# Linear attention followed by an MLP mixer on one core: the first channel product of 8 of 9 chunks in Strassen's form, smaller attention rings, new order lists

## The chip, the core and the metric

The kernel runs on one core of a Trainium2 chip. The core has five engines that take instructions from queues of their own, each queue in order: TensorE (PE, with its weight loads shown as PEld), VectorE (DVE), ScalarE (ACT), GpSimd (POOL) and SyncE (SP, here for issuing DMAs alone). Matrix products land in PSUM, of which there are eight banks of 128 partitions by 512 float32; DVE and ACT read PSUM, POOL is given SBUF operands only in this kernel. The metric is the device time in microseconds of one execution.

## What is computed

```python
def phi(x):                                   # x is q or k, scaled by D**-0.25
    h = einsum('bhsd,md->bhsm', x, omega) - sum(x*x, -1, keepdims=True)/2
    return exp(h - max(h, -1, keepdims=True)) / sqrt(m)
q_p, k_p = phi(q_s), phi(k_s)
kv, z = einsum('bhsm,bhsd->bhmd', k_p, v), sum(k_p, axis=2)
attn = einsum('bhsm,bhmd->bhsd', q_p, kv) / (einsum('bhsm,bhm->bhs', q_p, z)[..., None] + 1e-6)
x = attn.transpose(0, 2, 1, 3).reshape(B, S, H*D)          # 8 x 576 x 512
h = maximum(x^T @ w_tok1, 0) @ w_tok2                      # token mix, 576 -> 256 -> 576
u = x + h^T
out = u + maximum(u @ w_ch1, 0) @ w_ch2                    # channel mix, 512 -> 1536 -> 512
```

There are 8 batches, 8 heads, 576 rows, a head size of 64 and 128 features.

## The kernel before

**Tiling.** A batch has 576 rows: 512 main rows and a tail of 64. The channel mix works on nine chunks of 512 rows: chunks 0 to 7 are the main rows of the batches, chunk 8 (`c == B`) is the eight tails together. All matrix operands are float16, sums are float32 in PSUM.

**Attention** (`attention`, by head pairs `hp`). `kp` (L657) and `qp` (L669) make the projections into two banks each; ACT takes the exponential into `kp`, `qp` (L515). DVE takes the row maximum of the k features (`km`, L681) and its reciprocal (L683), POOL scales v by it (`vs`, L295), PE forms kv (L702 and, for the tails, L709 or L711), which is copied to `kvsb` (L286). `num` (L735, L737) is the product with q; DVE divides (L744, L745) and writes `x`. Batches 0 and 1 get q and k by PE transposes of rows loaded as they are; the others go through a DRAM scratch (POOL's DMA queue) and come back by transposing DMAs on SP's queue into the rings `qT` and `kT`.

**Token mix** (`token_mix`; `token_mix_first` for batch 0). Two products (L778, L791) with a ReLU between; DVE adds x into `u` (L794), and one transposing DMA on SP's queue (L799) makes `uT`, the moving operand of the channel mix.

**Channel mix** (`channel_mix`). The first product runs over 12 blocks of 128 columns of `w_ch1`: each block is four matmuls of 128x512 into one bank (L967) and one ReLU from PSUM into `r3`, on ACT (L290) or DVE (L292). The second product of chunks 1 to 8 is in Strassen's form already (`channel_out_fast`, seven products of half size, L917): DVE forms eight sums of `r3` a chunk (L295, 768 columns each), PE runs 84 matmuls of 128x256 a chunk, and DVE reads the banks X, Y, Z seven times into the float32 `o` (L906). Four combinations `T1..T4` of blocks of `w_ch2` are made once by DVE (L448). Chunk 0 is plain (L1001).

**Order and places.** Each piece of work is a job: an engine, a cost, a function, what it depends on and which ring places it takes and gives back. The list `ORDER` was written out beforehand: `Planner.run` calls the jobs in that order, so it fixes the order on every engine's queue. `SLOT` gives the place in a ring that each job takes (the eight PSUM banks are one such ring), `MOVED` says which jobs run on another engine than their usual one, and a negative number in `ORDER` is a matmul on zeros into a bank (L1039), done in the first microseconds only.

Of the kernel before, what the change touches and what calls it, by code (L numbers as in the profile page):

```python
# [9 lines left out]
FP32 = mybir.dt.float32  # L10
# [110 lines left out]
class Planner:  # L121
# [41 lines left out]
    def engine(self, usual):  # L163

        return MOVED.get(len(self.jobs), usual)
# [3 lines left out]
def kernel(  # L169
# [51 lines left out]
    NH = NCB // 2  # L221
    DH = DM // 2
    t_S = sb([P, 3, NH, 2 * P], FP16, "S")
    t_T = sb([P, 4, NH, DH], FP16, "T")
    early = t_S.rearrange("p a b c -> p (a b c)")
    zeros = early[:, 0:SM]
    ident32 = early[:, SM : SM + 2 * P].bitcast(FP32)
# [844 lines left out]
```

## Time and profile before

The time is 283.71 us, the median of three runs (283.15 to 284.58). One execution was profiled; its page gives a span of 281.1 us from the first to the last instruction. The page says nothing of that execution's time outside the span.

| | before |
|---|---|
| time, median of 3 runs | 283.71 us |
| span of the profiled execution | 281.1 us |
| instructions | 6278 |
| PE busy | 270.3 us, 96% |
| DVE busy | 222.4 us, 79% |
| ACT busy | 138.6 us, 49% |
| POOL busy | 92.0 us, 33% |
| DMA moved | 39.66 MB |

How to read it: busy time is the time in which at least one instruction of an engine was in work. A group of instructions is named by line, engine, operation, the tiles written and read, and shape; behind the count stand the busy time and the mean length of one in ns, then the idle time just ahead of them and who ended it. PE's matmuls are pipelined: the length of one is longer than the pace of many, so their pace is taken from a run of them in the chain of waits, which follows the work back from the last instruction.

### The profile page before, as it was taken

The page shows a single profiled execution, that of the slowest core. Times are in us where ns is not written, and L with a number is a line of the kernel's source. Part 1 is how long each engine was busy: PE and PEld are TensorE (multiplying, and loading weights), DVE is VectorE, ACT ScalarE, POOL GpSimd, SP SyncE. Part 2 cuts the span into 40 slices and gives each one's busy share as a digit, 9 for nine tenths or more (in the row PEclk, how much of TensorE's full clock was granted, in tenths as well). Part 3 has the DMA queues.
Part 4 walks back from the last instruction along what each step waited for, and adds up shares of the span by engine and source line. Part 5 has one row for each costly group of instructions (what it writes and reads, how often), then busy time and mean ns, then how long its engine had stood idle before and what let it go on. Part 6 is the DMA issues. An engine that isn't in the chain of part 4 may idle for free.

```text
span 281.1 us, 6278 instructions
## 1 busy us (share of the span) xinstructions
PE 270.3 (96%) x2526; PEld 167.6 (60%) x2526; DVE 222.4 (79%) x462; ACT 138.6 (49%) x288; POOL 92.0 (33%) x116
## 2 busy tenths in 40 slices
PE   6899999999999999999999999999999999999993
PEld 2547546443657755665667647755676467446782
DVE  2589828499999899996997999977995893565992
ACT  1498994049676418743758445734753510031200
POOL 8574994007510872048008710510033000000001
PEclk9999999999999999999999999999999999999999
DMA  6999999999998999997979993960151304030125
GB/s 161 194 189 161 157 169 213 178 191 202 179 218 184 148 172 186 181 198 104 212 178 185 241 135 101 161 156 2 76 97 59 111 0 96 0 149 2 75 90 135
DMA packets 80524, 39.66 MB, mean 141 GB/s; under 512 B 63984, under 2 KB 76016, under 8 KB 80304
## 3 DMA queue, kind: packets, MB, share of 16 engines
q0 software_dynamic: 31744, 17.74, 44.1%
q1 hardware_dynamic: 46832, 15.77, 29.1%
q10 hardware_dynamic: 1920, 5.77, 5.4%
q8 instruction: 19, 0.31, 0.4%
q14 instruction: 9, 0.07, 0.1%
HBM read 35.95 MB, written 16.52 MB: 187 GB/s over the span
## 4 chain that ended last, share of the span: by engine, by line
PE 89%; DVE 3%; DMA 2%; ACT 2%; issue 0%; SPq 0%; DVEq 0%
PE bank L967 32%; PE bank L917 26%; PE bank L791 5%; PE bank L778 5%; PE bank L1001 4%; PE bank L735 3%; PE bank L657 3%; PE bank L702 3%; DMA wc<-in_k_dram 2%; PE bank L669 2%; ACT kp L515 1%; PE bank L845 1%; PE bank L817 1%; PE bank L737 1%; PE bank L771 1%; DVE T L448 1%
## 5 line engine op out<-in xcount | busy, mean ns | idle before, releaser
L967 PE MATMUL bank<-uT,wc 128*128 128x512 f16 x376 | 89.6, 379 | 0.5 <-DVE r L292 0.4
L290 ACT ACTIVATE r<-bank 128x512 f16<-128x512 f32 (+1 forms) x86 | 47.7, 601 | 82.7 <-PE bank L967 61.5
L295 POOL TENSOR_TENSOR vs<-v,vs 128x512 f16<-128x512 f16 x32 | 34.2, 1072 | 94.4 <-DVE vs L683 51.3
L967 PEld LDWEIGHTS <-wc 128*128 128x128 f16 x424 | 38.8, 98 | 38.8 <-issue 1.6
L917 PEld LDWEIGHTS <-r 128*128 128x128 f16 x384 | 36.8, 98 | 8.2 <-issue 1.1
L515 ACT ACTIVATE kp<-bank 128x512 f16<-128x512 f32 x64 | 36.7, 618 | 8.9 <-PE bank L657 7.1
L515 ACT ACTIVATE qp<-bank 128x512 f16<-128x512 f32 x64 | 36.7, 614 | 8.8 <-PE bank L669 5.8
L681 DVE TENSOR_REDUCE km<-kp 128x8 f16<-128x1024 f16 x32 | 38.7, 1208 | 1.2 <-ACT kp L515 1.1
L292 DVE TENSOR_SCALAR r<-bank 128x512 f16<-128x512 f32 (+1 forms) x40 | 26.3, 670 | 15.7 <-PE bank L967 11.3
L745 DVE TENSOR_TENSOR x<-bank,rc 128x320 f16<-128x320 f32 x62 | 30.5, 492 | 2.1
L917 PEld LDWEIGHTS <-S 128*128 128x128 f16 x288 | 28.1, 98 | 5.8 <-issue 0.3
L906 DVE TENSOR_TENSOR o<-u,bank 128x512 f32<-128x512 f16 x28 | 19.0, 679 | 6.2 <-PE bank L917 5.8
L917 PE MATMUL bank<-T,r 128*128 128x256 f16 x192 | 23.8, 273 | 0.0
L917 PE MATMUL bank<-wc,r 128*128 128x256 f16 x192 | 23.6, 273 | 0.0
L917 PE MATMUL bank<-T,S 128*128 128x256 f16 x192 | 23.4, 273 | 0.0
L946 POOL DMA_DIRECT2D out_dram<-o x2 | 1.3, 645 | 61.2 <-issue 61.2
L906 DVE TENSOR_TENSOR o<-o,bank 128x512 f32<-128x512 f32 (+1 forms) x27 | 16.6, 617 | 2.5 <-PE bank L917 1.8
L735 PEld LDWEIGHTS <-qp 128*128 128x128 f16 x256 | 13.5, 98 | 8.1 <-DVE kvsb L286 0.7
L794 DVE TENSOR_TENSOR u<-x,bank 128x512 f16<-128x512 f16 x28 | 17.6, 680 | 0.0
L735 PE MATMUL bank<-kvsb,qp 128*128 128x65 f16 x256 | 15.0, 193 | 0.5 <-DVE kvsb L286 0.5
L791 PE MATMUL bank<-r,w 128*128 128x512 f16 x56 | 14.1, 381 | 0.0
L744 DVE RECIPROCAL rc<-bank 128x5 f32<-128x5 f32 x62 | 11.4, 184 | 2.9 <-PE bank L737 2.2
(119 smaller groups left out, 379.0 us busy)
## 6 DMA issues: line engine op xcount, KB each, us to landing
out_dram<-o ACTq DMA_DIRECT2D x9, 512.0 KB, 2.7
q<-in_q_dram POOLq DMA_DIRECT2D x6, 576.0 KB, 9.7
wc<-in_moe_w_ch_dram POOLq DMA_DIRECT2D x4, 768.0 KB, 9.0
k<-in_k_dram POOLq DMA_DIRECT2D x6, 512.0 KB, 7.8
v<-in_v_dram POOLq DMA_DIRECT2D x6, 512.0 KB, 9.9
out_dram<-o SPq DMA_DIRECT2D x5, 512.0 KB, 3.9
r<-in_q_dram POOLq DMA_DIRECT2D x4, 288.0 KB, 7.5
v<-in_v_dram POOLq DMA_DIRECT2D x4, 256.0 KB, 8.1
```

Of the source, the lines that this page charges most:

```text
L290: nc.scalar.activation(out=out, in_=in_, func=AF.Relu)
L292: nc.vector.tensor_relu(out=out, in_=in_)
L295: (nc.gpsimd if eng == "POOL" else nc.vector).tensor_tensor(**kw)
L515: nc.scalar.activation(out=out, in_=in_, func=AF.Exp, bias=0.0, scale=1.0)
L681: nc.vector.reduce_max(out=mx, in_=kpv, axis=AX.X)
L735: nc.tensor.matmul(ps[:, k, j * 65 : (j + 1) * 65], st, s[:, i, 0 : D + 1], start=True, stop=True)
L745: nc.vector.tensor_tensor(out=t_x[place("x", b)][:, :, (2 * hp + hs[0]) * D : (2 * hp + hs[0] + n) * D].rearrange("p j (i d) -> p i j d", ...
L791: nc.tensor.matmul(ps, w2_of(tb, j), r1[:, tb, :], start=(tb == 0), stop=(tb == NT - 1))
L794: nc.vector.tensor_tensor(out=t_u[place("u", b)][:, j, :], in0=t_x[place("x", b)][:, j, :], in1=bank(n), op=ALU.add)
L906: nc.vector.tensor_tensor(out=o, in0=a, in1=ps, op=ALU.add)
L917: nc.tensor.matmul(ps[:, j * DH : (j + 1) * DH], a[:, cb, j * P : (j + 1) * P], w[:, cb, :], start=(bank_of(b, j0) not in held and j == j0 ...
L967: nc.tensor.matmul(ps, wc1[:, db, cb * P : (cb + 1) * P], moving(db), start=(db == 0), stop=(db == ND - 1))
```

## The change

The first channel product of chunks 1 to 8 is put in Strassen's form as well (`channel_in_fast`). Rows and inner index are halved: `uT` gives four blocks, `w_ch1` gives four. Three sums of blocks of `uT` go to a new tile `V`, a fourth replaces a block of `uT`. For each of three groups `p` of two column blocks, seven products (28 matmuls of 128x256) go to three banks X, Y, Z. X is read three times on the way into float32 tiles `s` (ring of four), and three more instructions add `s` to a bank and write `r3`; the ReLU of these three quarters then runs in place on `r3`, the fourth quarter's reads the bank.

```diff
+def channel_in_fast(c, key, jt):
...
+    sums = {}
+    for n, what, op, after in (
+        (1, lambda: (v_of(0), u_of(0, 1), u_of(0, 0)), ALU.subtract, ()),
+        (2, lambda: (v_of(1), u_of(1, 1), v_of(0)), ALU.subtract, (1,)),
+        (4, lambda: (v_of(2), u_of(1, 0), v_of(1)), ALU.subtract, (2,)),
+        (3, lambda: (u_of(0, 1), u_of(1, 1), u_of(0, 1)), ALU.subtract, (1,)),
+    ):
...
+            o, a, b = what()
+            tt(e_sum, out=o, in0=a, in1=b, op=op)
+        sums[n] = add(e_sum, 1.0, key - 0.2, go_u, deps=[*jt, *[sums[x] for x in after]], take=[("V", c)], give=own)
+    ops = {
+        1: ("X", A11, lambda: u_of(0, 0), [], True), 2: ("Y", A12, lambda: u_of(1, 0), [], True),
+        6: ("X", S2, lambda: v_of(1), [sums[2], j_W[2]], False), 5: ("Z", S1, lambda: v_of(0), [sums[1], j_W[1]], True),
+        7: ("X", S3, lambda: u_of(0, 1), [sums[3], j_W[3]], False), 3: ("Z", S4, lambda: u_of(1, 1), [j_W[4]], False),
+        4: ("X", A22, lambda: v_of(2), [sums[4]], False),
+    }
+    for p in range(NH // 2):
...
+                ps, m = bank(bank_of(b)), moving()
+                for t in range(2):
+                    cb = 2 * p + t
+                    for k in range(2):
+                        nc.tensor.matmul(ps[:, 2 * P * t : 2 * P * t + 2 * P], a[:, k, cb * P : (cb + 1) * P], m[:, :, k, :],
+                                         start=(begin and t == 0 and k == 0), stop=False, skip_group_check=True)
...
+            def go_k():
+                copy(e_k, t_s[place("s", (c, p, x))].rearrange("p (t s) -> p t s", t=2), seen("X"))
...
+            def go_t():
+                nc.vector.tensor_tensor(out=rows(i, e), in0=t_s[place("s", (c, p, x))].rearrange("p (t s) -> p t s", t=2), in1=seen(b), op=ALU.add)
...
+        p1 = product(1, [])
+        ka = kept("a", [p1])
+        p2 = product(2, [])
+        p5 = product(5, [])
+        summed("a", "Y", 0, 0, [ka, p2], True)
+        p6 = product(6, [ka])
+        kb = kept("b", [p6])
+        p7 = product(7, [kb])
+        kc = kept("c", [p7])
+        t22 = summed("c", "Z", 1, 1, [kc, p5], False)
+        p3 = product(3, [t22])
+        summed("b", "Z", 1, 0, [kb, p3], True)
+        p4 = product(4, [kc])
...
+        def go_r(e_r=e_r, rows=rows, seen=seen):
+            relu_to(e_r, rows(0, 1), seen("X"))
...
+                x = t_r3[place("r3", c)][:, NH * e + part.start : NH * e + part.stop, 2 * P * i : 2 * P * i + 2 * P]
+                if e_p == "POOL":
+                    nc.gpsimd.tensor_scalar_max(out=x, in0=x, scalar1=0.0)
+                else:
+                    relu_to(e_p, x, x)
+    return ready
```

Weights: four combinations of `w_ch1` (`first_weights`: `S1`, `S2`, `S4` in a new tile `W`, `S3` over a block of `w_ch1`) and four of `w_ch2` (`second_weights`, `T3` now over a block of `w_ch2`), each one instruction of 1536 columns on DVE or POOL. Those that overwrite wait until chunk 0's plain products have read the block. `T1`, `T2` and `T4` lie where the masked v tails of batches 0 and 1 lay, and the sums for the second product lie where early constants lay; both now wait for those readers by dependencies of their own.

```diff
+def first_weights(plain):
+    for n, out_, a, b, op in ((1, S1, A21, A22, ALU.add), (2, S2, S1, A11, ALU.subtract), (4, S4, A12, S2, ALU.subtract), (3, S3, A11, A21, ALU.subtract)):
...
+            tt(e_w, out=o, in0=a, in1=b, op=op)
...
-        for g in range(2):
-            part = slice(g * NH // 2, (g + 1) * NH // 2)
+    PARTS = (slice(0, 4), slice(4, NH))
...
+        for g, part in enumerate(PARTS):
...
-                e_sum = engine("DVE")
+                e_sum = engine("DVE", "POOL")
```

The sums ahead of the second product are cut 1024 and 512 columns wide, not 768 and 768, may run on POOL, and each depends on the quarters of `r3` it reads, not on all. The rings of `qT`, `kT` and `v` go from three to two places, those of `qp` and `kp` from four to three; the load of `w_ch2` is written behind the first transposes of k, whose rows lie in its tile. `ORDER`, `SLOT` and `MOVED` are new throughout, so the DMAs on POOL's queue also stand in another order.

```diff
-    COUNT = {"qT": 3, "kT": 3, "v": 3, "vt": 2, "qp": 4, "kp": 4, "vs": 4, "qpt": 2, "kpt": 2, "vbd": 2,
-             "kvsb": 3, "ktt": 2, "x": 3, "r1": 3, "u": 3, "uT": 3, "r3": 2, "S": 1, "o": 2, "bank": 8}
+    COUNT = {"qT": 2, "kT": 2, "v": 2, "vt": 2, "qp": 3, "kp": 3, "vs": 4, "qpt": 2, "kpt": 2, "vbd": 2,
+             "kvsb": 3, "ktt": 2, "x": 3, "r1": 3, "u": 3, "uT": 3, "V": 1, "s": 4, "r3": 2, "S": 1, "o": 2, "bank": 8}
```

What the two programs hold, counted from their instructions:

| | before | after |
|---|---|---|
| matmuls, first channel product, chunks 1 to 8 | 384 of 128x512 | 672 of 128x256 |
| DVE: ReLU of 512 columns from PSUM (L292) | 38 | 11 |
| DVE: copies of a bank to `s`; `s` + bank to `r3` | 0; 0 | 12; 72 |
| DVE: sums for the second product | 64 of 768 | 7 of 1024, 14 of 512 |
| DVE: sums of blocks of `uT`; of weights (1536) | 0; 4 | 14; 4 |
| DVE: ReLU in place | 0 | 8 of 1024, 8 of 512 |
| ACT: ReLU of 512 from PSUM; copies to `s`; ReLU in place | 84; 0; 0 | 39; 60; 7 of 1024, 6 of 512 |
| POOL: sums for the second product | 0 | 25 of 1024, 18 of 512 |
| POOL: sums of blocks of `uT`; of weights (1536) | 0; 0 | 18; 4 |
| POOL: ReLU in place | 0 | 9 of 1024, 10 of 512 |
| POOL: v scaled (`vs`) | 32 | 31 (one on DVE) |

More of the change, by code (lines that the diff above doesn't have):

```diff
@@ L104 @@
+"ACT", 1432: "SP",
 }
@@ L490, in row_transposes @@
         for o in range(2):
-            eng = engine("ACT" if on_act else "DVE")
+            eng = engine(*("ACT", "DVE") if on_act else ("DVE", "ACT"))
             def rows_out(o=o, eng=eng):
@@ L543, in attention @@
         if b == 1:
-            e_ktt = engine("POOL")
+            e_ktt = engine("POOL", "DVE")
             def k_tails():
@@ L627, in attention @@
         if b == 0:
-            e_dup = engine("POOL")
+            e_dup = engine("POOL", "DVE")
             def qt_dup():
@@ L779, in token_mix @@
             j1 = add("PE", mm(4, 512), key + step * tb * 0.2, t1, deps=[jt, j_w1], take=[("r1", b)])
-            e_relu = engine("ACT" if tb == 0 or BY["re1"] == "A" else "DVE")
+            e_relu = engine("ACT", "DVE")
             def relu(tb=tb, n=n, e_relu=e_relu):
@@ L942, in channel_out_fast @@
                 for h in range(2):
[L943 removed]
+                    eng = engine(*("POOL", "ACT", "SP") if need == "22" else ("ACT", "SP") if h else ("SP", "ACT"))
                     def store(i=i, j0=js[0], js=slice(*js), cols=cols, h=h, eng=eng):
@@ L957, in moving @@
+    def channel_mix(c, key, jt):
+        if c == NPE - 1:
+            first_weights(j_plain["in"])
+            second_weights(j_plain["out"])
+        if c >= NPE - 1:
+            channel_out_fast(c, key, channel_in_fast(c, key, jt))
+            return
         def moving(db):
-            return (t_uT[place("uT", c)] if c < B else uTt)[:, :, db, :]
+            return t_uT[place("uT", c)][:, :, db, :]
         jr = [None] * NCB
-        fast = c >= NPE - 1
-        order = [x for i in range(NH) for x in (i, i + NH)] if fast else range(NCB)
@@ L962, in channel_mix @@
-        for pos, cb in enumerate(order):
+        j_plain.update({"in": [], "out": []})
+        for pos, cb in enumerate(range(NCB)):
             n = ("h3", c, cb)
@@ L980, in channel_mix @@
                 j1 = add("PE", mm(4, 512), key + 0.5 * pos / NCB, c1, deps=[*jt, j_wc1[cb // (NCB // 2)], *first], take=[("bank", n), ("r3", c)],
-                       give=[("uT", c)] if c < B else [])
+                       give=[("uT", c)])
             j1.heavy = True
-            e_relu = engine("ACT" if c >= NPE or BY[("r0", "r1")[c]][cb] == "A" else "DVE")
+            j_plain["in"].append(j1)
+            e_relu = engine("ACT", "DVE")
             def relu(cb=cb, n=n, e_relu=e_relu):
@@ L1003, in channel_mix @@
                            deps=[prev, *jr[4 * part : 4 * part + 4], *j_wc2], take=[("bank", n)], give=[("r3", c), ("uT", c)])
+                j_plain["out"].append(prev)
             k2 = key + 0.5 + 0.5 * (3 * j + 3) / 12
-            e_out = engine("DVE")
+            e_out = engine("DVE", "ACT")
             def out_copy(j=j, n=n, e_out=e_out):
```

176 lines of the change are left out of this document (117 added, 59 removed), and 110 rows, old and new, of the table ORDER.

## The prediction

> **What bounds the kernel now.** I read the page's busy times first, then the chain of waits, then busy times by stretch.
>
> ```profile
> PE 270.3 (96%) x2526; PEld 167.6 (60%) x2526; DVE 222.4 (79%) x462; ACT 138.6 (49%) x288; POOL 92.0 (33%) x116
> PEclk9999999999999999999999999999999999999999
> ...
> PE 89%; DVE 3%; DMA 2%; ACT 2%; issue 0%; SPq 0%; DVEq 0%
> PE bank L967 32%; PE bank L917 26%; PE bank L791 5%; PE bank L778 5%; PE bank L1001 4%; PE bank L735 3%; PE bank L657 3%; PE bank L702 3%; DMA wc<-in_k_dram 2%; PE bank L669 2%; ACT kp L515 1%; PE bank L845 1%; PE bank L817 1%; PE bank L737 1%; PE bank L771 1%; DVE T L448 1%
> ```
>
> TensorE is busy 96% of the span at the full granted clock and makes up 89% of the chain that ended last; a third of the chain is the line that the change rewrites, L967. VectorE is second, 79% in the mean. A mean hides stages, so I asked for stretches: the head, the middle up to the last batch's `u`, its fullest 30 us, the last stretch and the end.
>
> ```profile
> core 0: us, PE busy (x) PEld busy (x) DVE busy (x) ACT busy (x) POOL busy (x), PEclk, DMA share, GB/s
> 0.00:33.50 33.50, 28.23 (x398) 17.31 (x399) 22.68 (x57) 22.71 (x55) 23.91 (x37) 1.00 1.05 172
> 65.00:95.00 30.00, 29.59 (x286) 18.49 (x286) 28.33 (x53) 21.14 (x44) 11.45 (x14) 1.00 1.07 188
> 230.00:276.40 46.40, 46.23 (x330) 31.99 (x327) 31.24 (x59) 5.92 (x11) 1.28 (x2) 1.00 0.22 68
> 276.40:281.10 4.70, 0.00 (x0) 0.00 (x0) 0.29 (x1) 0.00 (x0) 0.00 (x0) 0.88 0.51 142
> 33.50:230.00 196.50, 195.79 (x1800) 118.30 (x1800) 168.22 (x348) 109.98 (x223) 66.79 (x78) 1.00 0.89 153
> ```
>
> In the middle PE never rests (195.79 of 196.5 us) and DVE has 168.22, or 86%; in the fullest 30 us DVE stands at 28.33, or 94%, with PE still at 99%. So PE sets the pace, and DVE has only 28 us to spare over the whole middle. That reserve decides this case.
>
> **What it takes from PE.** The pace of matmuls comes from long unbroken runs in the chain:
>
> ```profile
> 238.88 13.81 PE bank L967 x64
> ...
> 265.73 10.52 PE bank L917 x96
> ```
>
> ```profile
> L967 PE MATMUL bank<-uT,wc 128*128 128x512 f16 x376 | 89.6, 379 | 0.5 <-DVE r L292 0.4
> L917 PEld LDWEIGHTS <-r 128*128 128x128 f16 x384 | 36.8, 98 | 8.2 <-issue 1.1
> ```
>
> A 512-column matmul costs 13.81/64 = 0.2158 us, a 256-column one 10.52/96 = 0.1096 us. The change takes out 384 x 0.2158 = 82.9 us and puts in 672 x 0.1096 = 73.6 us: 9.2 us less on PE. There are 288 more weight loads, but one takes 98 ns, under the 109.6 ns of the matmul that hides it, and L917's run shows that pace with one load per matmul. If that cover were gone, each load would show in full (28 us), which L917 excludes. PE alone would give 281.1 - 9.2 = 271.9 us of span.
>
> **What it gives to DVE.** DVE instructions overlap at their ends, so I take their pace from the gaps between starts in a stretch without idle time:
>
> ```profile
> 225.93 0.56 DVE L295 TENSOR_TENSOR S<-r,S 128x768 f16<-128x768 f16 x1
> 226.40 0.55 DVE L295 TENSOR_TENSOR S<-S,r 128x768 f16<-128x768 f16 x1
> ...
> 226.93 0.69 DVE L906 TENSOR_TENSOR o<-u,bank 128x512 f32<-128x512 f16 x1
> 227.53 0.55 DVE L295 TENSOR_TENSOR S<-r,S 128x768 f16<-128x768 f16 x1
> 228.00 1.87 DVE L794 TENSOR_TENSOR u<-x,bank 128x512 f16<-128x512 f16 x3
> ```
>
> Three PSUM sums of 512 columns take 1.87 us, 0.62 each; a sum of 768 columns in SBUF takes 0.47 to 0.53, say 0.50, or 0.65 us per 1000 columns.
>
> ```profile
> L292 DVE TENSOR_SCALAR r<-bank 128x512 f16<-128x512 f32 x38 | 25.5, 684 | 15.2 <-PE bank L967 11.3 <-PE bank L778 3.6
> L906 DVE TENSOR_TENSOR o<-o,bank 128x512 f32<-128x512 f32 x21 | 14.1, 674 | 1.9 <-PE bank L917 1.3 <-issue 0.3
> L448 DVE TENSOR_TENSOR T<-wc,T 128x1536 f16<-128x1536 f16 x2 | 2.7, 1362 | 0.0
> L394 DVE CAST ident<-S 128x128 f16<-128x128 f32 x1 | 0.2, 226 | 0.2 <-POOL S masks.py:199 0.2
> ```
>
> Taken out: 27 ReLUs x 0.62 = 16.7; 64 sums x 0.50 = 32.0; the four `T` at 5.5 (two at 2.7, two alike); three copies moved away, about 1.9. Together 56.1 us. Put in: 72 sums of `s` and a bank, float32 like the `o` row, x 0.62 = 44.6; 12 copies x 0.62 = 7.4; 7 sums of 1024 (0.67) and 14 of 512 (0.33), 9.3; 14 sums of `uT` blocks x 0.33 = 4.6; four weight sums x 0.93 = 3.7; two moved instructions, 1.0; and 16 ReLUs in place. No row has such a ReLU: one 16-bit SBUF input. The cast of 128 columns (0.226) bounds it below; the two-input sum, scaled, bounds it above at 0.67 and 0.33. I take 0.25, near the row with one input: 4.0 us (3.6 to 8.0). Together 74.6, so DVE rises by 18.5 to 240.9 us. The Trainium skill ("VectorE: DVE Perf Modes", the perf-mode tier table) lets such an instruction move four elements a cycle, which by its cycle formula is an estimated 0.33 and 0.19 us; the sixteen would then come to 4.2. No run here shows it.
>
> ACT loses 45 ReLUs and gets 60 copies and 13 ReLUs in place, about 28 instructions of 0.6 us more, some 20 us at 49%: not a bound. The wait is another matter: within a group of columns PE's products 6, 7, 4 wait for ACT's copy of X, product 3 for a DVE sum, and all later matmuls queue behind. Other groups and the second product lie between, so I charge nothing while ACT and DVE are on time; whatever DVE is late by, PE is late by.
>
> **Where DVE then sets the pace.** Behind the issue of the last batch's transposing of `u` the new order leaves 476 matmuls of 256 columns, 476 x 0.1096 = 52.2 us for PE, and for DVE 33 PSUM sums or copies, 29 sums into `o`, 20 small ones, about 45 us: there PE leads. Ahead of it stand 240.9 - 45 = 196 us of DVE work, 22.7 of it in the head. So 173.3 us of DVE stand in the middle, where PE's own time falls from 196.5 by the 9.2 and by the 5.8 that the last stretch is longer (52.2 against 46.4), to 181.5. DVE would have to be busy 95% of it, fuller than the fullest 30 us of before, for 180 us on end, both queues in order and each waiting for the other.
>
> **The shared resource.** POOL's vector work is 34.2 + 6.3 + 1.9 + 1.9 = 44.3 us now, 16% of the span.
>
> ```profile
> L295 POOL TENSOR_TENSOR vs<-v,vs 128x512 f16<-128x512 f16 x32 | 34.2, 1072 | 94.4 <-DVE vs L683 51.3 <-PE bank L669 22.2 <-PE bank L917 13.8
> L295 POOL TENSOR_TENSOR vbd<-vt,vbd 128x512 f16<-128x512 f16 x6 | 6.3, 1053 | 20.4 <-DVE vbd L594 17.7 <-DMA vt<-in_v_dram 2.6
> L295 POOL TENSOR_TENSOR T<-vt,T 128x1024 f16<-128x1024 f16 x1 | 1.9, 1937 | 0.0
> L295 POOL TENSOR_TENSOR T<-vt,mask 128x1024 f16<-128x1024 f16 x1 | 1.9, 1904 | 0.0
> L546 POOL COPY ktt<-kT 128x256 f16<-128x256 f16 x1 | 0.4, 390 | 3.9 <-DVE kT L286 3.9
> ```
>
> Added: 36 sums of 512 x 1.07 = 38.5; 25 of 1024 x 1.92 = 48.0; four of 1536, by that slope 2.8, 11.2; 19 ReLUs between the copy row scaled (0.78 and 1.56) and the sum rows (1.07 and 1.92): the copy has one input, so 0.8 and 1.4, 20.6. That is 118 us; POOL stands at 210 us, its vector work at 162, or 58%. Now what happens where DVE and POOL both work on SBUF:
>
> ```profile
> 64.51 0.91 DVE L448 TENSOR_TENSOR T<-wc,T 128x1536 f16<-128x1536 f16 x1
> 65.33 1.81 DVE L448 TENSOR_TENSOR T<-wc 128x1536 f16<-128x1536 f16 x1
> ...
> 64.85 1.48 POOL L295 TENSOR_TENSOR vs<-v,vs 128x512 f16<-128x512 f16 x1
> ...
> 20.62 0.83 DVE L631 COPY qpt<-qpt 128x512 f16<-128x512 f16 x1 [0.49 <-ACT qpt L515]
> ...
> L594 DVE TENSOR_TENSOR vbd<-rct,mask x6: 193/195/465, 63.0 to 208.6; 128x8 f16<-128x8 f16 x6
> ```
>
> The POOL instruction that starts in the first `T` takes 1.48, not 1.07; the second `T`, started while POOL works, takes 1.81 against 0.91, as if it began when POOL ended; one of six `vbd` has 0.465 against 0.195. After the change 56 DVE instructions have two SBUF inputs or copy within SBUF. If they fall blindly, 58%, or 32, meet a POOL instruction (125 of 1.29 us) and wait half of one: 32 x 0.64 = 21 us. Before, 75 at 16% would make 12 meetings, and 4 are long: a `T` in each of its two groups (the mean of 1362 ns is half of 0.91 + 1.81), one `vbd`, and the copy of `qpt`, 0.83 us for 512 columns. That is a third. I take a third, 7 us, and keep 0 and 21 as ends. The Trainium skill ("SBUF — State Buffer", the section on SBUF's two separate sides) states the rule that speaks against this change: a DVE instruction with two SBUF inputs, or in a two-port mode, and a GpSimd instruction exclude each other for their whole length. The `T` rows agree; the rule counts every meeting, which gives the 21.
>
> **What costs nothing.** Two places for `qT`, `kT`, `v` instead of three: a batch takes 196.5/7 = 28 us, and the transposing DMA 6.8 us to land, so it still fits while one batch is read; without cover 6.8 us a batch. The smaller `qp`, `kp` rings: ACT's exponentials start later, and ACT has room. POOL's DMA issues now stand behind 80 more vector instructions, some of which wait for DVE, but the loads are for a batch ahead, 28 us. `w_ch2` behind the first transposes: its tile holds k's rows, so it waited before as well. In the head, batch 0's second half of v goes from the 7th to the 16th DMA on POOL's queue, about 1.5 MB more ahead of it, 8 us at the 172 GB/s of the head; its third scaling ran at 18.64, and DMAs in between were earlier loads of batch 1 that fill PE and DVE meanwhile. I take 0, with -2 and +4 as ends.
>
> ```profile
> kT<-k SPq DMA_TRANSPOSE x6, 6.8
> ```
>
> ```profile
> 18.64 1.05 POOL L295 TENSOR_TENSOR vs<-v,vs 128x512 f16<-128x512 f16 x1 [1.59 <-DVE vs L683]
> ```
>
> **The sum.** Head 33.5, middle (173.3 + 7)/0.93 = 193.9, last stretch 52.2, end 4.7: a span of 284.3. The 0.93 lies between 0.86 (all of the middle, where DVE was not the bound) and 0.94 (the fullest stretch), nearer to that. The median of the runs lies 283.7 - 281.1 = 2.6 above the profiled span, so 286.9, say 287 us: PE's 9.2 us are given back as waiting for DVE, and about 3 more.
>
> **Rivals.** (1) PE keeps the pace, DVE is always just in time: 271.9 + 2.6 = 274.5, up to 282 where it is partly so. For it: 94% beside a full PE has been seen, and no sum for the second product met POOL before: the sixteen of the row below have a mean of 551 ns, and the single ones above 0.55 or 0.56. It decides if collisions stay under 3 us and DVE over 94%: 33.5 + 173.3/0.944 + 56.9 + 2.6 = 276.6. Against it: 190 us of that. (2) Every meeting is paid, 21 us: 33.5 + 194.3/0.93 + 56.9 + 2.6 = 302. For it: POOL works in bursts on the same sums as DVE. Against it: POOL's chains depend on DVE's results, so they often alternate. (3) The new products don't reach 109.6 ns, since a moving operand of two strips of 128 columns is new: at 82.9/672 = 0.123 us nothing is saved, the time is 283.7 and whatever DVE adds, 284 to 292. Nothing speaks for it but its novelty.
>
> ```profile
> L295 DVE TENSOR_TENSOR S<-r 128x768 f16<-128x768 f16 x16 | 8.8, 551 | 0.6 <-ACT r L290 0.4
> ```
>
> **How the numbers follow.** DVE sets the pace with some collisions (281 to 295): 0.46. Rival 1: 0.34. Rival 2: 0.17. Rival 3: 0.03. A measurement of this kernel can tell 0.5% (282.3 to 285.1) from no change. Of the first case 0.04 lie below that, 0.10 within, 0.32 above. So faster 0.38, the same 0.10, slower 0.52. The range of 274 to 300 leaves out the worst of rival 2 and little else.
>
> **What would show it.** Right: DVE busy over 90% in the middle, idle PE ahead of L1020 released by DVE or ACT, two-input sums on DVE of 1 to 2 us beside POOL's. Wrong: PE at 99% of the middle with the span near 272; or DVE's total far from 241; or a head much longer than 33.5.

## The result and the profile after

The changed kernel takes 354.04 us, the median of four runs (350.08 to 363.42), beside 283.45 us for the one before (four runs, 283.15 to 284.58): 1.235 times as long, 95% interval 1.231 to 1.239. Two of the four runs, 357.27 and 363.42, were disturbed and are not in the ratio, and below "after" is the other two, 350.08 and 350.82, in the middle 350.4 us; of three experiments (a_head, a_apart, a_reluact) one run of two was disturbed, the one profiled, and the other's time is given. The forecast was 287, so it missed by some 63 us, outside its range. The profiled execution is the one of 350.08 us, with a span of 348.1.

The page of the changed kernel, busy times, granted clock in 40 slices, and the chain that ended last:

```profile
PE 285.3 (82%) x2814; PEld 205.0 (59%) x2814; DVE 269.9 (78%) x503; ACT 158.8 (46%) x319; POOL 240.1 (69%) x200
...
PEclk9669879999699989965899789999996999999999
...
PE 32%; DVE 27%; POOL 13%; DMA 12%; issue 10%; ACT 4%; DVEq 0%; POOLq 0%; ACTq 0%
```

No engine is full any more. PE fell from 96% to 82% of a longer span and from 89% of the chain to 32%. The rest is shared by DVE, POOL, DMA and "issue": no single new bound, but engines that wait for each other in turn. PE's busy time rose by 15 us although it has less to do; the clock row says why, since slices at 0.5 to 0.8 stretch the matmuls: 285.3 times the mean clock of 0.912 is 260.2, beside 270.3 before less the forecast's 9.2.

Where it idles shows in the busy times by stretch (columns as in the prediction: PE, weight loads, DVE, ACT, POOL, then clock, DMA share, GB/s):

```profile
core 0: us, PE busy (x) PEld busy (x) DVE busy (x) ACT busy (x) POOL busy (x), PEclk, DMA share, GB/s
0.00:33.50 33.50, 25.32 (x347) 15.88 (x348) 18.64 (x50) 19.96 (x49) 28.03 (x44) 0.80 1.10 181
33.50:50.00 16.50, 10.01 (x106) 6.86 (x104) 7.64 (x16) 7.90 (x17) 7.87 (x9) 0.79 1.38 142
...
82.00:101.00 19.00, 9.87 (x61) 4.61 (x59) 8.94 (x14) 8.10 (x17) 4.07 (x5) 0.82 1.21 202
...
142.00:163.00 21.00, 8.79 (x101) 6.57 (x100) 9.08 (x18) 5.72 (x14) 11.56 (x7) 0.71 1.39 117
...
300.00:343.40 43.40, 38.98 (x345) 33.24 (x344) 38.61 (x62) 10.14 (x17) 37.61 (x23) 1.00 0.15 57
```

Three stretches, 33.5 to 50, 82 to 101 and 142 to 163, hold 27.8 of PE's 62.8 idle us. In them PE is busy 42 to 61% of the time, DVE and ACT 27 to 48%, and the DMA share is over 1.2; what they wait for is shown next. In the last 43 us it is another picture, DMA share 0.15, DVE at 89% and POOL at 87% beside a PE at 90%. These are the two halves of what follows.

PE's own waits (line waited at, who ended it: us in total, times, longest), and five pieces of the chain (start, length, what):

```profile
PE bank L567 <- DMA kT<-k: 11.8, 2, 10.7
PE bank L684 <- DMA qT<-q: 7.7, 2, 6.2
PE bank L717 <- POOL vs L292: 7.7, 2, 6.4
...
PE bank L1020 <- DMA uT<-u: 2.6, 1, 2.6
```

```profile
28.87 14.02 DMA v<-in_v_dram
...
82.26 14.89 issue
...
141.96 20.65 DMA qT<-q
...
189.24 4.76 DVE r L289
...
254.41 5.51 POOL r L1062 x2
```

The first three pieces are the three stretches: a load of v that takes 14 us, a wait that the chain calls "issue", and a transposing DMA of 20.65 us. The middle one is a transfer too: it ends at 97.15, where POOL starts its first sum of `uT`. POOL's row of the waits says for whom it stood there:

```profile
POOL V L292 <- DMA uT<-u: 19.3, 2, 14.9
```

The stages of the forecast's sum can be laid beside each other, since their borders can be found in every trace: the head ends with the first plain product of chunk 0 (L1084), the middle with the issue of the last batch's transposing DMA of `u`, the last stretch with PE's last matmul. The three right-hand columns are experiments of the next section.

| us | forecast | after | a_noload | a_pool8 | a_noload_pool8 |
|---|---|---|---|---|---|
| head | 33.5 | 49.9 | 41.7 | 53.8 | 41.7 |
| middle | 193.9 | 236.3 | 209.0 | 210.6 | 188.2 |
| last stretch | 52.2 | 57.8 | 57.8 | 52.0 | 52.1 |
| end | 4.7 | 4.2 | 4.6 | 4.4 | 4.8 |
| span | 284.3 | 348.1 | 313.0 | 320.8 | 286.8 |

### The profile page after: what moved, and what is told of

Same layout as the page of the kernel before. It is cut to its first block, busy times and chain, and to the rows that moved or that the text cites. A ratio compares the mean times of both kernels' runs of the same rounds, so it can differ in the third digit from the quotient of the medians.

```text
span 348.1 us, 7081 instructions
## 1 busy us (share of the span) xinstructions
PE 285.3 (82%) x2814; PEld 205.0 (59%) x2814; DVE 269.9 (78%) x503; ACT 158.8 (46%) x319; POOL 240.1 (69%) x200
## 4 chain that ended last, share of the span: by engine, by line
PE 32%; DVE 27%; POOL 13%; DMA 12%; issue 10%; ACT 4%; DVEq 0%; POOLq 0%; ACTq 0%
PE bank L935 12%; PE bank L1020 8%; DMA qT<-q 6%; DVE r L1033 5%; DVE o L924 4%; DMA v<-in_v_dram 4%; DVE km L696 3%; DVE r L289 3%; POOL r L1062 3%; POOL S L292 3%; DVE S L292 3%; DVE x L762 2%; DMA r<-in_q_dram 2%; PE bank L1084 2%; POOL W L292 2%
## 5 line engine op out<-in xcount | busy, mean ns | idle before, releaser
L283 ACT COPY s<-bank 128x512 f32<-128x512 f32 x60 | 33.9, 589 | 63.5 <-PE bank L1020 43.4
L1033 DVE TENSOR_TENSOR r<-s,bank 128x512 f16<-128x512 f32 x72 | 47.5, 679 | 16.0 <-PE bank L1020 13.3
L1062 POOL TENSOR_SCALAR r<-r 128x512 f16<-128x512 f16 (+1 forms) x19 | 40.0, 2108 | 27.1 <-DVE r L1033 27.0
L292 POOL TENSOR_TENSOR vs<-v,vs 128x512 f16<-128x512 f16 x31 | 33.1, 1074 | 33.4 <-DVE vs L698 20.3
L1020 PEld LDWEIGHTS <-wc 128*128 128x128 f16 x384 | 36.6, 98 | 15.1 <-issue 5.4
L1020 PE MATMUL bank<-uT,wc 128*128 128x256 f16 x252 | 35.6, 275 | 5.7 <-DMA uT<-u 2.6
L935 PE MATMUL bank<-wc,r 128*128 128x256 f16 x288 | 38.7, 290 | 0.8 <-DVE o L924 0.8
L935 PEld LDWEIGHTS <-S 128*128 128x128 f16 x288 | 27.9, 100 | 11.0 <-issue 4.7
L1020 PEld LDWEIGHTS <-W 128*128 128x128 f16 x288 | 27.6, 98 | 7.9 <-issue 2.2
L287 ACT ACTIVATE r<-bank 128x512 f16<-128x512 f32 (+1 forms) x41 | 23.9, 593 | 16.5 <-PE bank L1020 7.4
L1020 PE MATMUL bank<-V,W 128*128 128x256 f16 x192 | 27.7, 273 | 0.9 <-DVE r L1033 0.6
L292 POOL TENSOR_TENSOR S<-r,S 128x1024 f16<-128x1024 f16 (+1 forms) x15 | 25.6, 1717 | 0.1
L292 POOL TENSOR_TENSOR r<-r 128x1024 f16<-128x1024 f16 (+1 forms) x10 | 20.1, 2012 | 3.6 <-DVE S L292 3.1
```

Of the source, the lines that this page charges most:

```text
L283: (nc.scalar.copy if eng == "ACT" else nc.vector.tensor_copy)(out=out, in_=in_)
L287: nc.scalar.activation(out=out, in_=in_, func=AF.Relu)
L292: (nc.gpsimd if eng == "POOL" else nc.vector).tensor_tensor(**kw)
L935: nc.tensor.matmul(ps[:, j * DH : (j + 1) * DH], a[:, cb, j * P : (j + 1) * P], w[:, cb, :], start=(bank_of(b, j0) not in held and j == j0 ...
L1020: nc.tensor.matmul(ps[:, 2 * P * t : 2 * P * t + 2 * P], a[:, k, cb * P : (cb + 1) * P], m[:, :, k, :], start=(begin and t == 0 and k == 0 ...
L1033: nc.vector.tensor_tensor(out=rows(i, e), in0=t_s[place("s", (c, p, x))].rearrange("p (t s) -> p t s", t=2), in1=seen(b), op=ALU.add)
```

## The experiments

Two theories stood against each other. *Loads*: q and k of batches 2 to 7 arrive late. *POOL*: the new vector work on POOL is slower than priced and holds up DVE on their common way to SBUF. A third, *clock*, says that PE's half clock after each idle time costs the time. Each expectation is quoted as it was on record before its run. Line numbers shift by a few lines from kernel to kernel.

### The rings alone, in the kernel before

```diff
-    COUNT = {"qT": 3, "kT": 3, "v": 3, ...
+    COUNT = {"qT": 2, "kT": 2, "v": 3, ...
```

> The kernel before with two places instead of three for qT and kT, nothing else changed. Theory R (the smaller rings make the transposing DMAs late): the ring place of batch b-2 has to be released first, so the span grows by 10 to 20 us of the 67, to 291 to 301 us. Rival (the rings are innocent, since the places are released at least 6 us of TensorE work before they are taken again): 282 to 286 us.

Measured: 283.96 us (10 runs, 282.89 to 285.71), ratio 0.999 (0.996 to 1.002). Two places for `qT` and `kT` cost nothing while the old order stands.

### Without the loads of q and k

```diff
 def cast(...)  # and cast_main, cast_tail, back (the transposing DMA)
-    nc.gpsimd.dma_start(out=scratch[w, b]..., in_=src[w][b]...)
+    pass
```

> The changed kernel without the loads of q and k for batches 2 to 7 (no copies to the DRAM scratch, no transposing DMAs into qT and kT; these batches read the rows of batches 0 and 1 again). Theory L (late loads, and the half clock that follows an idle TensorE): the idle time ahead of L567 and L684 (19.5 us), the one ahead of L717 in the head (6.4), part of the one ahead of the first L1020, and most of the half-clock stretches go: 300 to 320 us. Theory V (vector work of DVE and POOL sets the pace): no vector instruction has gone, so over 335 us.

Measured: 315.15 us (315.13 to 315.16), 35 less than after. Much, but 28 more than forecast: loads are not all. The edit also takes 24 DMA issues off POOL, whose busy time falls by 15 us (240.1 to 224.9), so the 35 us can hold a part that is POOL's.

### Without the ReLUs in place

```diff
             def go_n(part=part, i=i, e=e, e_p=e_p):
-                x = t_r3[place("r3", c)][...]
...
+                pass
```

> The changed kernel without the 48 in-place ReLUs on r3 (the second channel product reads three quarters of r3 unclipped in chunks 1 to 8): 40.0 us less on POOL, 17.3 on DVE, some 9 on ACT. Theory V: 25 us or more off, under 325 us. Theory L: the waits for loads stay, 335 to 347 us.

Measured: 340.46 us (338.76 to 342.17), 10 less, as the loads theory had it.

### PE kept busy

Before nine matmuls that had long waits, 162 matmuls of 512 columns go into the bank that the waiting one overwrites, so that the clock has no reason to fall.

```diff
+FILL = {237: 27, 552: 26, 853: 46, 864: 5, 901: 18, 1239: 7, 1215: 5, 315: 10, 45: 18}
...
+            for _ in range(FILL.get(n, 0)):
+                self.keep(self.held[next(x for x in j.take if x[0] == "bank")], n)
```

> The changed kernel with 162 matmuls of 512 columns added, on resident data, into the bank that the waiting matmul overwrites right after, at nine places where TensorE stood idle for 1 to 10 us. No wait is removed; TensorE only stays busy in it. If the half clock after idle time costs what the trace says (285.3 us busy at a mean clock of 0.912 is 260 us at full clock, so 25 us), the time falls by 10 to 20 us, to 330 to 340. If the other engines set the pace after each wait anyway, it stays at 346 to 354.

Measured: 354.78 us (353.62 to 355.94). Its page:

```profile
PE 312.4 (88%) x2976; PEld 215.1 (61%) x2976; DVE 269.9 (76%) x503; ACT 158.7 (45%) x319; POOL 240.0 (68%) x200
...
PEclk9967998999999999999899899999999999999999
```

Most slices now have the full clock (mean 0.971 for 0.912), and the time is not better. So the half clock isn't what makes the 63 us. That a gain of some us is hidden here, because the added matmuls outlast some of the waits, this run doesn't exclude; a_pool8 below is 28 us faster at nearly the clock of after, 0.917.

### POOL's new work made small

From chunk 2 on POOL's sums, and all its ReLUs, handle 8 columns; number, order and waits of the instructions stay.

```diff
+                    if e_sum == "POOL" and c > 1:
+                        o, a, b = o[:, 0, 0:8], a[:, 0, 0:8], b[:, 0, 0:8]
...
-                        nc.gpsimd.tensor_scalar_max(out=x, in0=x, scalar1=0.0)
+                        nc.gpsimd.tensor_scalar_max(out=x[:, 0, 0:8], in0=x[:, 0, 0:8], scalar1=0.0)
```

> The changed kernel with POOL's new vector instructions cut to 8 columns each: all 19 in-place ReLUs, and from chunk 2 on the sums of uT blocks and the sums for the second product that run on POOL (the rest of their columns is not computed). Every instruction, wait and queue place stays. POOL falls from 240 to about 125 us and DVE's in-place ReLUs and SBUF sums lose their collisions, about 20 us. Theory V (the vector work and its collisions cost what exceeds my forecast): 310 us or less. Theory L (late loads cost over half of it, and vector work the rest): 325 to 335 us.

Measured: 322.52 us (322.43 to 322.61), 28 less than after.

### Both together

> Both at once: no loads of q and k for batches 2 to 7, and POOL's new vector instructions cut to 8 columns. If late loads and POOL's work with its collisions together are the whole miss, what is left is the DVE-paced kernel of the forecast, 282 to 295 us. If the new order costs by itself (engines that wait for each other in queue order with nothing late), it stays over 300 us.

Measured: 288.95 us (288.71 to 289.19). Alone the two give 35.3 and 27.9 us, together 61.5: they add up almost, and together they are as large as the miss. The page's busy times and the stretches of this kernel:

```profile
PE 269.2 (94%) x2814; PEld 199.3 (69%) x2814; DVE 246.5 (86%) x505; ACT 158.1 (55%) x319; POOL 116.1 (40%) x176
```

```profile
0.00:41.70 41.70, 34.05 (x449) 21.43 (x449) 26.07 (x66) 27.65 (x65) 30.65 (x45) 0.84 0.97 162
41.70:230.00 188.30, 183.22 (x1898) 131.92 (x1895) 175.16 (x357) 114.92 (x229) 78.20 (x106) 1.00 0.39 76
230.00:282.10 52.10, 51.93 (x472) 45.99 (x472) 44.97 (x84) 15.51 (x27) 7.23 (x26) 1.00 0.24 74
```

PE leads the last stretch, 51.93 of 52.10 us, and in the middle PE stands at 97% beside a DVE at 93%.

### The issue order in the head

The first 36 DMA issues on POOL's queue are put in the order of their first need, in the places that DMA issues had; the rest of the list stays.

```diff
-... -1, 12, 23, 2, 32, 16, 14, 26, 21, 0, 1, ...
+... -1, 12, 10, 2, 32, 16, 14, 7, 21, 0, 1, ...
```

> The changed kernel with the first 36 DMA issues on POOL's queue put in the order in which the list of jobs first needs them (v of batch 1 and the weights ahead of the copies to scratch for batches 2 and 3); all else stays. The 14 us landing of v that held the head goes: if the head's 16 us were lost to the order of the issues alone, 335 to 342 us; if the first 50 us are short of transfer rate whatever the order (the attention of batch 2 is asked for 25 us of TensorE work earlier than before), within 4 us of the changed kernel, 346 to 354.

Measured: 359.02 us, one run. Not better, rather worse: this order doesn't help. Others weren't tried.

### A list made anew with POOL's measured prices

Jobs, engines and ring sizes stay; `ORDER` and `SLOT` are made again, by a list scheduling that takes POOL's durations from the trace of after.

```diff
-ORDER = [...]
+ORDER = [...]
```

> The same jobs on the same engines with the same rings, in an order list that I made from the old one: each engine takes, in simulated time, the first job of the list that is ready, with POOL's instructions priced at what this trace shows (in-place ReLU 2.7 and 1.4 us, sums 2.1 and 1.1) and not at the costs that stand in the jobs. Theory O (the list was laid out for other durations, so queues stand behind jobs that come late): 20 us less, 325 to 335 us. Theory L or V alone: the work and the transfers are the same, so within 5 us, 345 to 355.

Measured: 364.29 us (362.83 to 365.75). This tells of that one list only; it doesn't show that no order does better.

### Fewer loads

First the copies to scratch of batches 3 to 7 are left out, with the transposing DMAs kept; then the loads of batches 2 and 3 alone.

```diff
 def cast(...)  # and cast_main, cast_tail
+    if b > 2:
+        return
...
-    nc.sync.dma_start_transpose(out=t.unsqueeze(1), in_=scratch[w, b])
+    nc.sync.dma_start_transpose(out=t.unsqueeze(1), in_=scratch[w, 2])
```

> The changed kernel without the copies of q and k to the DRAM scratch for batches 3 to 7 (POOL's queue); the transposing DMAs of all batches stay and read batch 2's scratch. Theory L1 (the transposing DMAs land late because they share the transfer engines with the copies, and wait for them): their landing falls from 12 us to about 6, and the time comes within 6 us of the run without any loads of q and k (315): 312 to 321 us. Theory L2 (they are late where they stand in SP's queue, behind waits for ring places and outputs): most of the loss stays, 335 to 350 us.

```diff
 def cast(...)  # and cast_main, cast_tail, back
+    if b < 4:
+        return
```

> The changed kernel without the loads of q and k for batches 2 and 3 alone (these two read the rows of batches 0 and 1 again); batches 4 to 7 load as before. If the loss to loads is made in the first 100 us, where the DMA rate is full: 25 to 35 us off, 318 to 328. If it is made anew at every batch (the 10.7 us wait for kT at 148 us is batch 5's): 10 to 15 us off, 335 to 343.

Measured: 325.88 us (324.45 to 327.31) and 335.01 (333.02 to 337.01). Without the copies the transposing DMAs land, in the median, about as they did before the change (6.8 for `kT`); with them it takes 1.6 and 2 times as long. The page's DMA rows (last number: median us from issue to landing), after and without copies:

```profile
kT<-k SPq DMA_TRANSPOSE x6, 12.1
qT<-q SPq DMA_TRANSPOSE x6, 11.8
```

```profile
kT<-k SPq DMA_TRANSPOSE x6, 7.7
qT<-q SPq DMA_TRANSPOSE x6, 5.8
```

So the copies on POOL's queue that belong to other batches, mere neighbours, make the transposing DMAs late; the next experiment shows it without leaving anything out. Without the loads of batches 2 and 3 the time falls by 15 us, as the expectation has it for a loss that is made anew in later batches: batch 4's pair then takes 23 to 25 us to land, batch 5's 24 and 11. SP's queue in after shows the same (start, time held, what):

```profile
28.50 4.31 SPq L377 DMA_TRANSPOSE kT<-k  x1
32.93 16.15 SPq L377 DMA_TRANSPOSE qT<-q  x1
...
93.27 3.85 SPq L377 DMA_TRANSPOSE kT<-k  x1
97.23 2.63 SPq L377 DMA_TRANSPOSE qT<-q  x1
...
141.96 16.82 SPq L377 DMA_TRANSPOSE qT<-q  x1
```

Those at 32.93 and 141.96 were issued with copies and loads of the next batches in flight and held SP's queue for 16 us; from issue to landing they took 23.6 and 20.65. Those at 93.27 and 97.23 had next to none beside them: 6.5 and 4.9. Not every overlap costs as much: in the kernel before, a transposing DMA of `kT` at 74.39 had five other transfers issued behind it and landed in 8.9 us. What makes the difference no run shows.

### Copies kept apart from transposing DMAs

The copies of batch b wait until both transposing DMAs of batch b-1 have landed, from batch 3 on, and stand correspondingly later on POOL's queue.

```diff
+        landed = [ld[w + "T", b - 1] for w in "qk"] if b > NPE else []
...
-            casts[w].append(dma("POOL", key + 0.01 * n, 3.2, ..., deps, cost=0.55))
+            casts[w].append(dma("POOL", key + 0.01 * n, 3.2, ..., [*deps, *landed], cost=0.55))
```

> The changed kernel with the copies of q and k to scratch for batch b (3 to 7) moved on POOL's queue to where TensorE first reads batch b-1, and made to wait until batch b-1's two transposing DMAs have landed, so that no such copy is in flight beside them, as in the kernel before. Theory L3 (a transposing DMA that runs beside copies takes about 20 us for both, alone 5 to 6: the overlap is the loss): the transposing DMAs land in 8 us or less, and 15 to 25 us come back: 326 to 337. Theory L4 (the new list reads each batch earlier than the transfers can bring it, whatever they run beside): the copies are now late in place of the transposing DMAs, 345 us or more.

Measured: 339.26 us. The landings in its DMA rows and the first two of its SP queue:

```profile
kT<-k SPq DMA_TRANSPOSE x6, 7.9
qT<-q SPq DMA_TRANSPOSE x6, 6.7
```

```profile
29.17 10.33 SPq L396 DMA_TRANSPOSE kT<-k  x1
39.62 17.82 SPq L396 DMA_TRANSPOSE qT<-q  x1
```

The delay is gone for batches 3 to 7, some 11 us of time with it, though nothing was left out: less than the 15 to 25 us expected, and from one run. Batch 2's pair still takes 24 and 30 us to land, beside the loads of v and `w_ch2`. The new order puts 437 matmuls ahead of PE's first reading of batch 2's `kT`, the old one 602; by their columns, at 0.2158 us for 512, that is some 24 and 50 us of PE work. So the next run takes batch 2's loads away as well:

```diff
+                if b == 2:
+                    return
```

> a_apart without the loads of q and k of batch 2 (it reads batch 0's and 1's rows again): the only transposing DMAs that still ran beside copies there, 24 and 30 us from issue to landing, because the list has TensorE read batch 2 ahead of the first channel product while v of batch 1 and the weights are still coming. If that early demand is the rest of the loss to loads (342 against 315): 318 to 328 us. If the rest is spread over the later batches: 333 to 340.

Measured: 325.98 us (325.31 to 326.64), 13 less again. To 315.15, with no load at all, 11 us remain that no run divides further; what POOL's DMA issues cost, which a_noload leaves out, may be among them.

### The ReLUs on ACT

All 48 in-place ReLUs go to ACT, first alone, then with the copies kept apart.

```diff
-MOVED = {... 331: "POOL", 332: "POOL", ... 491: "POOL", 492: "POOL", ...
+MOVED = {... 328: "ACT", 330: "ACT", 331: "ACT", 332: "ACT", ... 489: "ACT", 491: "ACT", 492: "ACT", ...
```

> The changed kernel with all 48 in-place ReLUs on ACT (19 came from POOL, 16 from DVE), at their places in the list. POOL 40 us less, DVE 17 us less, ACT some 28 us more, 187 of 350. If their length on POOL and DVE was what they cost, the time comes to that of the kernel without them, 338 to 345. If ACT, in order, now brings the copies s late behind ReLUs that wait for DVE: 350 us or more.

> Both of these edits together. If the two losses are separate, as the runs without loads and without POOL's work said (315 and 322, both 289): the sum of the two gains, 312 to 325 us. If one edit only uncovers the other's wait: no better than the better of the two.

Measured: 375.13 us, and 361.47 (360.88 to 362.06): worse by some 25 and 22 us, although ACT had half its time free. Two of its waits:

```profile
POOL S L298 <- ACT r L293: 60.6, 9, 18.6
...
ACT r L293 <- DVE r L1039: 24.5, 17, 3.2
```

ACT waits 17 times for the DVE sum ahead of a ReLU, and in its queue the copies to `s` and the exponentials stand behind that; POOL's sums wait 60.6 us for the ReLUs. DVE was busy 256.3 us instead of 269.9, and nothing came of it. Here free time on an engine was no room for an instruction whose input comes late, in an order that was made for another engine.

### POOL's two kinds of work apart

With the loads out, once the ReLUs are left out and once the sums are made small (the edits of above).

> The changed kernel without the loads of q and k for batches 2 to 7 and without the 48 in-place ReLUs: which part of POOL's 26 us (315 to 289) is the ReLUs. If it is their 40 us on POOL with the wait for them: 290 to 297. If it is POOL's sums and their collisions with DVE as much: 300 to 306.

> The changed kernel without the loads of q and k for batches 2 to 7, and from chunk 2 on with POOL's sums (of uT blocks and for the second product) cut to 8 columns; the in-place ReLUs whole. The counterpart of a_noload_norelu (302). If sums and ReLUs cost separately, the 26 us of POOL's work less the ReLUs' 13 are the sums': 299 to 304. If POOL only needs to be less full, either way, so that each alone would have sufficed: under 296.

Measured: 302.19 us (302.05 to 302.32) and 294.34 (294.29 to 294.38), from 315.15: 13 for all the ReLUs, 21 for POOL's sums, and 26 for sums and POOL's ReLUs together. They overlap: each is partly hidden behind the other. In the last stretch it is the sums alone: without them it takes 52.1 us, without the ReLUs 57.6 of 57.8.

### The form where it has room: two chunks only

The kernel before, with the new first product in chunks 7 and 8 alone: their batches need no more loads, the tiles `W`, `V` and `s` fit into places of `qT`, `kT` and `v` that have had their last readers, ReLUs go to ACT, and the list is the old one up to its entry 889.

```diff
+        if c >= 7:
+            if c == 7:
+                first_weights(xs[5], j_plain)
+            channel_out_fast(c, key, channel_in_fast(c, key, jt))
+            return
```

> The kernel before with the first channel product in Strassen's form for the last two chunks alone, where its DVE was busy 31 of 46 us and nothing is loaded any more; V, s and the weight sums lie in the qT, kT and v places of batches 5 and 6, so no ring is smaller; the list is the old one up to its 889th entry, with the end listed anew. TensorE: 96 matmuls of 512 columns out, 168 of 256 in, 20.7 - 18.4 = 2.3 us less. If the end keeps TensorE fed: 281 to 282.5 us, 0.4 to 0.9% faster than before. If the longer chain of a chunk (sums of uT, product, copy, sum, ReLU, sums, product) leaves TensorE waiting at the end: 284 to 288.

Measured: 283.51 us (12 runs, 281.96 to 284.97) beside 284.56 for the kernel before (17 runs): ratio 0.997 (0.994 to 0.9996). That is 0.3% faster, its interval barely short of no change and less than the 0.4 to 0.9% expected: as good as the same. Its page:

```profile
PE 268.5 (95%) x2598; PEld 174.5 (62%) x2598; DVE 231.1 (82%) x486; ACT 149.3 (53%) x307; POOL 101.8 (36%) x121
```

PE has 1.8 us less than before, about 1 of which arrives at the end of the run.

## Why the prediction was wrong, by its steps

**PE's term, 9.2 us: right.** With loads and POOL's work away, the last stretch took 52.1 us for the forecast's 52.2, at full clock. Rival 3 falls with one row of after's chain, 12 matmuls in 1.31 us, or 109 ns each:

```profile
329.04 1.31 PE bank L1020 x12
```

**"What costs nothing": failed, and worth about 35 us.** The ring argument held for `qT` and `kT` (those rings alone: 284 us; the smaller `v`, `qp` and `kp` no run tests alone). But the sentence that "the transposing DMA 6.8 us to land, so it still fits" took the landing of before as a constant. In the new order copies run beside the transposing DMAs of three of the six batches, and these then take 18 to 24 us; and the order asks for batch 2 some 25 us of PE work earlier. I had looked at how many DMAs stand in a queue and not at which of them fly at the same time, nor at when PE first reads each batch. Landing and first need together were the step to take. Of the 35 us, a_apart shows some 11 for the neighbours of batches 3 to 7 and a_apart_no2 some 13 for batch 2; 11 stay undivided. The Trainium skill ("DMA: Bandwidth & Descriptors", rules for kernel authors) says that a transpose next to ordinary DMAs needs nothing; that is said of the data, and for the time these runs show otherwise.

**The head, 33.5 us (-2 to +4): failed by 16.** 8 of them go with the loads (41.7). The other 8 stay in a_noload_pool8. There 449 matmuls stand ahead of the border where before it was 398, but the 51 have 5607 columns, 2.4 us at 0.2158 us for 512. PE is busy 34.05 us there for 28.23; what the 51 don't explain of that goes with the granted clock, 0.84 for 1.00. PE's longest wait there is one of 3.7 us, for rows of q. What holds up the head wasn't settled; a_head shows no more than that one other order of POOL's issues doesn't help.

**POOL's 210 us: 240.1.** The bounds for its in-place ReLU came from a copy and a sum, and I took 0.8 and 1.4. In after (partitions x elements, count, busy, mean ns):

```profile
L1062 POOL TENSOR_SCALAR r<-r 128x1024 f16<-128x1024 f16 x9 | 25.2, 2801 | 10.5 <-DVE r L1033 10.4
L292 POOL TENSOR_TENSOR S<-S,r 128x1024 f16<-128x1024 f16 x5 | 10.7, 2130 | 0.8 <-DVE S L292 0.7
L1062 POOL TENSOR_SCALAR r<-r 128x512 f16<-128x512 f16 x10 | 14.8, 1483 | 16.6 <-DVE r L1033 16.6
L292 POOL TENSOR_TENSOR V<-uT,V 128x512 f16<-128x512 f16 x8 | 9.3, 1165 | 0.4
```

2.80 and 1.48 us lie above both bounds: 40.0 us for 20.6. The sums took 13% more than priced, some 13 us in all.

**Collisions, "a third, 7 us": failed.** DVE was busy 269.9 us, and 247.9 with POOL's work made small: 22 us, three times the 7. The DVE rows of one and the same ReLU, in after and with small POOL instructions:

```profile
L289 DVE TENSOR_SCALAR r<-r 128x1024 f16<-128x1024 f16 x8 | 9.0, 1129 | 0.1
L289 DVE TENSOR_SCALAR r<-r 128x512 f16<-128x512 f16 x8 | 8.3, 1033 | 0.1
```

```profile
L289 DVE TENSOR_SCALAR r<-r 128x512 f16<-128x512 f16 x8 | 3.5, 435 | 0.1
L289 DVE TENSOR_SCALAR r<-r 128x1024 f16<-128x1024 f16 x8 | 3.4, 425 | 0.1
```

0.43 us for 1.03 and 1.13. So an instruction with one SBUF input meets POOL as well, as the Trainium skill says of a two-port mode ("SBUF — State Buffer", SBUF's two separate sides). The prediction had the rule and discounted it by three, since before had four long cases where it expected twelve meetings. That was the wrong reading: in before only 3 of the 75 two-input instructions start while POOL is in vector work, and all 3 are long (the fourth long case was a copy). Meetings were rare in that order, not cheap. In after 26 of DVE's 63 instructions of these kinds (47 sums and products with two SBUF inputs, 16 ReLUs in place) start while a two-input instruction of POOL runs, and 25 of them take over 1.3 times the shortest of their shape in any run.

It matters what POOL does. 11 more start while POOL's in-place maximum (its ReLU) runs, and 7 of them stay within 1.3 times the shortest. A ReLU of each kind, and what POOL had in work, shows the difference:

```profile
255.44 0.42 DVE L289 TENSOR_SCALAR r<-r 128x1024 f16<-128x1024 f16 x1
...
262.11 1.78 DVE L289 TENSOR_SCALAR r<-r 128x512 f16<-128x512 f16 x1
```

```profile
254.41 5.50 POOL L1062 TENSOR_SCALAR r<-r 128x1024 f16<-128x1024 f16 x2 [5.38 <-DVE r L1033]
...
261.62 2.12 POOL L292 TENSOR_TENSOR S<-S,r 128x1024 f16<-128x1024 f16 x1 [0.69 <-DVE S L292]
```

The ReLU of 1024 columns takes 0.42 us inside POOL's maximum; the one of 512 takes 1.78 us beside a sum, and ends 0.15 us after it. So the rule that the prediction cites for every GpSimd instruction holds here for POOL's sums, and for its maximum in 4 cases of 11.

That the 22 us lie so near rival 2's 21 is luck. 10.4 of them are the 16 ReLUs, which are not among the instructions that rival counted with two SBUF inputs or as copies; the rest, 11.4, is the two-input instructions, of which it counted 56 and the trace has 47. Its 302 us lie 13 short of a_noload's 315, where the loads are out. DVE's own 240.9 was nearly right: 246.5 to 247.9 are measured, with a few meetings left in them, and the ReLU, 0.43 for 0.25, explains 2.9 of the difference.

The place of the loss was not DVE's queue alone either, as rival 2 has it. POOL's ReLUs are in the chain themselves (5.51 us at 254.41), and in the last stretch, where "there PE leads" was the forecast, POOL's work, its sums, cost 5.7 us (57.8, and 52.1 without it). POOL's part of the miss, 26 to 28 us, is collisions and waiting for POOL's slower results together; no run divides the two.

**The signs that were named.** "DVE busy over 90% in the middle" did not come (191.2 of 236.2 us, 81%), "idle PE ahead of L1020 released by DVE or ACT" hardly (its largest wait there is for `uT`, 2.6 us); "two-input sums on DVE of 1 to 2 us" did, and so did one of the signs against it, the long head. The sum's pace, DVE at 0.93 of the middle, no run confirms: without loads and POOL's work DVE does fill 93%, but beside a PE at 97%, so DVE need not be what sets the pace there. That this run's 288.95 us lie near the 287 is an accident: its head is 8.2 us longer than forecast and its middle 5.7 us shorter, and it hardly has the collisions for which the forecast holds 7 us.

## What to carry to other kernels

When a change comes with a new order, check for each transfer when it is first needed and which other transfers are in flight with it, ahead of any sum over engines: a landing time read from the old order holds for the old neighbours only. Sums given to POOL are paid twice where DVE works in SBUF at the same time, once as POOL's own long instruction and once as DVE's wait. Count the meetings of DVE's instructions from SBUF to SBUF, those with one input too, with POOL's two-input instructions, and price every one; that few met in the old order says nothing of the new. And a kernel whose PE is 96% busy has room for fewer matmuls only where the other engines and the transfers have room at that very place: here, of what was tried, two chunks of eight.

## What was unexpected of the hardware

- Transposing DMAs issued beside plain copies in after took 18 to 24 us to land and held the issuing queue up to 16.8 us; with next to none beside them 4.5 to 6.5.
- DVE's instructions from SBUF to SBUF were held up by POOL's two-input instructions (25 of 26 that started in one), and by POOL's in-place maximum in 4 cases of 11 only.
- POOL's in-place maximum with a constant (2.80 us for 1024 columns) is slower than its sum of two inputs (2.13).
- One in-place ReLU on DVE lasted 4.85 us, more than ten times its own 0.43. DVE's row and POOL's in the same time:

```profile
189.15 4.85 DVE L289 TENSOR_SCALAR r<-r 128x1024 f16<-128x1024 f16 x1
```

```profile
188.84 1.06 POOL L292 TENSOR_TENSOR vs<-v,vs 128x512 f16<-128x512 f16 x1
189.84 0.70 POOL L348 DMA_DIRECT2D vt<-in_v_dram  x1
190.57 1.07 POOL L292 TENSOR_TENSOR vs<-v,vs 128x512 f16<-128x512 f16 x1
191.58 2.12 POOL L292 TENSOR_TENSOR S<-r 128x1024 f16<-128x1024 f16 x1
```

It began during one sum of POOL, and ended 0.3 us after the third was over: two POOL instructions that started later went first. The gap at 189.9 to 190.6, in which POOL only issued a DMA, was not enough for it to get in; why, no run shows.
